# Strided sparse attention with an MLP: loads, scores, half sums and V copies of chunk 1 in another order

## The chip, the core and the metric

The kernel runs on one core of a Trainium2 chip. The metric is the device time of one execution in microseconds. The engines are named as in the profile: PE (matrix multiplies; PEld its weight loads), DVE (vector), ACT (scalar, activations), POOL (GpSimd), SP (it issues DMAs). DMAs issued by POOL go through its software queue, DMAs issued by SP through a hardware queue.

## The reference

Inputs are q, k, v of shape (8, 8, 576, 64) in float32, weights w_in (512 x 2048) and w_out (2048 x 512), and alpha (2048). What matters of the computation:

```python
scores = q @ k.transpose(0, 1, 3, 2) / sqrt(64)
mask_local   = (rel >= 0) & (rel < 32)                      # heads 0 to 3
mask_strided = (rel >= 0) & (pos_k % 32 == pos_q % 32)      # heads 4 to 7
attn = softmax(where(mask, scores, -1e9)) @ v
x = attn.transpose(0, 2, 1, 3).reshape(4608, 512)
h = x @ w_in
out = (maximum(h, 0) + alpha * minimum(h, 0)) @ w_out
```

## The kernel before

The work is one stream on PE with two strands. One strand is the MLP in 9 chunks of 512 tokens (chunk 0 is planned separately). The other is the attention of 32 pairs of heads: pair g belongs to batch g // 4; the first two pairs of a batch are local, the last two strided. The attention of batch n + 1, and the start of the batch after it, runs in between the matmuls of chunk n.

For a pair there are these pieces. T turns q and k of the two local pairs of a batch (PE transposes by identity, copies on ACT). For strided pairs, and from batch 2 on, q and k are loaded in their order by `load_d` (POOL's queue, tiles `qsd` and `ksd`) and turned by `transpose_d` with DMA transposes on SP. S, `score_both`, computes the scores of the pair in two halves: 12 or 16 matmuls into PSUM tiles (`sp`, `sph`), an exp on ACT for each (L400, L406; the exps of the second half are deferred to this and the next attention step), and a multiplication with the mask (L402, L409), on POOL except for pair 11, whose masks run on DVE. P, `pv_piece`, multiplies a group with V (L430), and DVE divides by the row sums (L437, L439) into `x` or `x16s`. P(g, a) is group a of pair g. X, `x_dma` and `x_copy` bring the result into `xT`: by DMA transposes for local pairs and for the first strided pair of a batch (into `xs` first, L469, from which ACT copies, L478), by PE transposes for the second strided pair.

PSUM is tight: the tiles with tag `ps` (T's results, `sph`, `pv`) share three buffers, so a piece may wait until ACT or DVE has read an earlier one.

In chunk n >= 1 the loop at L942 has 30 slots i. Slots 0 to 15 are up-projection blocks, `lin1_piece`: four matmuls of 512 columns into `hps` (L613), ACT's relu into `neg` (L621), DVE's combination into `gT` (L624). Slots 16 to 29 are down-projection blocks, `lin2_fast`: eight matmuls of 256 columns each. They use a fast scheme with seven products instead of eight, which needs sums of halves of `gT` (`g_sum`, L653, tiles `gsum`) and of w_out (`wout_sum`, tiles `wsum`). After each block, `attn_n(cnt, ab)` takes `cnt` attention pieces from the list built at L501 to L575, then the half sums of that slot are issued. For chunk 1 `cnt` and the sums (`early`, L928) are written out by hand, and so are the loads of batch 3 and the copies of its strided V: `load_v(3, False)` fills `vl`, `load_v(3, True)` fills `stv`, `cast_v` copies `stv` to `vs` on POOL, `cast_l` casts q and k on ACT or POOL. `load_d(3)` comes from the list of pieces, behind the last P of group 10.

In chunk 1 the order before is: slot 0 Tq and slot 1 Tk (pairs 8, 9), slot 4 S(8), 6 S(9), 9 P(8,0), 11 P(8,1), 13 P(9,0), 14 S(10), 15 P(9,1), 16 S(11), 17 P(10,0), 18 Tq (pairs 12, 13), 19 P(10,1), 20 Tk, 21 P(10,2), 22 S(12), 23 P(11,0) and so on. P(9,0) stands ahead of S(10) because of L523.

Ahead of chunk 1 stands chunk 0's down-projection, an order written out by hand at L913 to L918: U(kf) multiplies row block kf of w_out into three banks, W(i) does two row blocks for the fourth. U(8) is the first that needs the third quarter of w_out.

Of the kernel before, what the change touches and what calls it, by code (L numbers as in the profile page):

```python
# [32 lines left out]
def kernel(  # L33
# [13 lines left out]
    B, H, S, D = q.shape  # L47
# [36 lines left out]
    DX = 2  # L84
# [404 lines left out]
    def T(u, nm):  # L489
        return lambda: transpose_piece(u, nm)  # L490
# [4 lines left out]
    def Pv(g, i):  # L495
        return lambda: pv_piece(pairs[g], i)

    def X(g, eng=None):
        return lambda: x_piece(pairs[g], eng or ("act" if pairs[g].strided else "dve"))

    for g in range(7, npair + 2):  # L501
        c = g // 4
        a, p, t = g, g - 1, g + 1
        okA = 8 <= a < npair
        okP = 8 <= p < npair
        okT = 8 <= t < npair and t < 4 * NX and (t % 4 == 0 or t < 4 * DX and t % 2 == 0)
        nP = len(pairs[p].pgroups) if okP else 0
        seq = []
        if okA:
            seq.append(("S", lambda a=a: score_both(pairs[a])))  # L510
        if okP:
            seq.append(("P", Pv(p, 0)))
        if okT:
            seq.append(("T", T(t // 2, "q")))
        if 8 <= g - 2 < npair and not pairs[g - 2].xd:
            seq.append(("X", X(g - 2)))
        if okP:
            seq.append(("P", Pv(p, 1)))
        if okT:
            seq.append(("Tk", T(t // 2, "k")))  # L520
        if nP == 3:
            seq.append(("P", Pv(p, 2)))
        if g == 10:  # L523
            seq[0], seq[1] = seq[1], seq[0]
        if not seq:
            seq.append(("N", lambda: None))

        todo = [(c, pr) for pr in range(2)] if g % 4 == 0 and 8 < g < npair else []

        if g % 4 == 1 and 9 <= g and c + 1 < B:  # L530
            todo = [(c + 1, nm) for nm in "qk"]
        lastP = max([i for i, z in enumerate(seq) if z[0] == "P"], default=len(seq) - 1)
        nslots = [i for i, z in enumerate(seq) if z[0][0] != "S"] or list(range(len(seq)))
        for i, (kind, fn) in enumerate(seq):
            extra = []
            if todo and i in nslots:
                left = len([z for z in nslots if z >= i])
                cnt = -(-len(todo) // max(1, left))
                extra = [todo.pop(0) for _ in range(min(cnt, len(todo)))]

            def run(fn=fn, extra=extra, g=g, c=c, kind=kind, lastp=(i == lastP), first=(i == 0),
                    second=(i == min(1, len(seq) - 1))):
                fn()
                for b, pr in extra:
                    if pr in ("q", "k"):
                        if b == 3:
                            continue
                        if b < NX:
                            cast_l(b, pr)
                        if b + 1 < NX:  # L550
                            load_qk(b + 1, pr)
                        continue
                    if b == 3:
                        continue
                    cast_v(b, pr, "pool")
                    if pr == 1 and b + 1 < B:
                        load_v(b + 1, True)
                if first and g % 4 == 2 and NX <= c + 1 < B:
                    turn_rows(c + 1)
                if lastp and g % 4 == 3 and NX <= c + 2 < B:  # L560
                    load_rows(c + 2, "k")
                if lastp:
                    if 4 * DX <= g - 1 < npair and pairs[g - 1].xd:
                        x_dma(pairs[g - 1])
                    if g % 4 == 3 and DX < c + 1 < B:
                        transpose_d()
                    if g % 4 == 2 and DX <= c and c + 1 < B:
                        load_d(c + 1)
                    if g % 4 == 1 and DX < c and c + 1 < B:
                        load_v(c + 1, False)  # L570
                    if g % 4 == 1 and NX <= c + 2 < B:
                        load_rows(c + 2, "q")
                if second and 4 * DX <= g - 3 < npair and pairs[g - 3].xd and pairs[g - 3].strided:
                    after.append(lambda: x_copy(pairs[g - 3]))
            feed(run, g - 2 if kind == "X" else -1)  # L575
# [247 lines left out]
    def ov(b, eng, c0, c1):  # L823
        return lambda: over_v(b, eng, c0, c1)
# [54 lines left out]
    def U(kf):  # L879
        def run():  # L880
            if kf == 0:
                banks.extend(phpool.tile([128, 512], F32, tag="hps", name="ops") for _ in range(3))
            for mt in range(3):
                keep(nc.tensor.matmul(  # L884
                    banks[mt], gTs[0][:, kf, 128 * mt : 128 * mt + 128], wout16[:, kf, :],
                    start=(kf == 0), stop=(kf == 15)))
            if kf == 15:
                for mt in range(3):
                    osb = opool.tile([128, 512], F32, tag="osb", name="osb")
                    cast_copy("dve" if mt == 1 else "act", osb, banks[mt])  # L890
                    keep(nc.sync.dma_start(out[128 * mt : 128 * mt + 128, :], osb))
        return run

    def W(i):
        def run():
            if i == 0:
                ops_cur["t"] = pspool.tile([128, 512], F32, tag="ps", name="ops")
            for kf in (2 * i, 2 * i + 1):
                keep(nc.tensor.matmul(  # L899
                    ops_cur["t"], gTs[0][:, kf, 384:512], wout16[:, kf, :], start=(kf == 0), stop=(kf == 15)))  # L900
            if i == 7:
                osb = opool.tile([128, 512], F32, tag="osb", name="osb")
                keep(nc.scalar.copy(osb, ops_cur["t"]))
                keep(nc.sync.dma_start(out[384:512, :], osb))
        return run

    def ws(z):
        return lambda: wout_sum(z, "dve", 0)

    def sc1(g, eng="dve"):  # L910
        return lambda: score_both(pairs[g], eng)

    for fn in [  # L913
        vs(1, 0, "pool"), sc1(6), U(0), vs(1, 1, "pool"), U(1), sc1(7), U(2), U(3), Cl(1, "q", "act"), Pv(6, 1),
        Cl(1, "k"), Pv(6, 2), Pv(6, 0), U(4), U(5), Pv(7, 0), Pv(7, 1), U(6), loads2, T(2, "q"), U(7), Pv(7, 2), W(0), W(1),
        T(2, "k"), U(8), X(7, "act"), U(9), ws(0), ws(1), ws(2), W(2), sc1(4), W(3), ov(1, "dve", 0, 24), U(10), sc1(5, "pool"), W(4), U(11),
        X(6, "act"), Pv(4, 1), W(5), Cl(2, "q", "act"), Cl(2, "k", "act"), U(12), Pv(4, 0), U(13), Pv(5, 0), U(14), Pv(5, 1),
        U(15), W(6), X(4, "dve"), X(5, "dve"), W(7)]:  # L918
        fn()
    for z in range(3):  # L920
# [5 lines left out]
    load_qk(3, "k")  # L926

    early = {  # L928
        11: [(0, 0, "pool")], 16: [(0, 1, "dve"), (1, 0, "dve")], 18: [(1, 1, "dve"), (2, 0, "dve")],
        20: [(2, 1, "dve"), (3, 0, "dve")], 22: [(3, 1, "dve")]}  # L930
    sums = {
        5: [(2, 0, "pool")], 9: [(0, 0, "pool")], 16: [(0, 1, "dve"), (1, 0, "dve")],
# [5 lines left out]
    for n in range(1, NCH):  # L938
        ab = attn_until(n + 1) if n + 1 < B else len(pieces)
        left = ab - pos["i"]  # L940
        acc = 0.0
        for i in range(30):  # L942
            if i < 16:
                lin1_piece(n, 8 * (i // 8) + 2 * (i % 4) + i % 8 // 4)
            else:
                lin2_fast(n, i - 16)
            if n == 1:
                cnt = int(i > 12 or i in (0, 1, 4, 6, 9, 11))
            else:
                acc += left / (19.5 if n == B - 2 else 21) * (0.5 if i < 16 else 1.0)  # L950
                cnt = int(acc)
                acc -= cnt
            attn_n(cnt, ab)
            for z, h, eng in {1: early, 2: sums2}.get(n, sums).get(i, ()):
                g_sum(n, z, h, eng)
            if n > 1:
                continue
            if i == 7:
                for pr in range(2):
                    cast_v(2, pr, "pool")  # L960
                    load_qk(4, "qk"[pr])
            if i == 15:
                load_v(3, False)
                load_v(3, True)
                cast_l(3, "q", "act")
            if i == 17:
                cast_l(3, "k", "act")
            if i == 28:
                for pr in range(2):
                    cast_v(3, pr, "pool")  # L970
                load_v(4, True)
        while pos["i"] < ab:
            attn_step(ab)
# [30 lines left out]
```

## Time and profile before

| what | value |
| --- | --- |
| runs | 300.34, 298.74, 298.70 us; median 298.74 |
| profiled execution | 298.81 us, its span in the profile 296.9 us |
| granted TensorE clock | 0.999 |
| busy share of the span | PE 98%, PEld 63%, DVE 73%, ACT 61%, POOL 62% |
| DMA | 41.18 MB in 97488 packets, mean 139 GB/s |
| the chain that ended last, by engine | PE 75%, DMA 13%, DVE 5%, ACT 2%, POOL 2% |

A timeline row of the profile reads: start in us, time in us, engine, line, operation, out<-in, shapes, count; in brackets the idle time of that engine just before and what ended it. Times of matmuls overlap, since they are pipelined and their ends are modelled. L numbers are lines of the kernel before.

### The profile page before, as it was taken

What the parts mean: (1) busy time and instruction counts of PE and PEld (TensorE: products, weight loads), DVE (VectorE), ACT (ScalarE), POOL (GpSimd) and SP (SyncE); (2) the same over time, 40 slices, a digit from 0 to 9 for tenths busy, and PEclk for the clock granted to TensorE, in tenths of its full rate; (3) what the DMA queues carried; (4) which work ended last, traced back from release to release, by engine and by line L of the source; (5) the groups of instructions that cost most, each with busy time, mean ns of one, the idle gap of its engine ahead of it and who ended that gap; (6) DMA issues with size and microseconds to landing.
All of it is one profiled execution on the core that took longest, in us unless ns stands there. A gap on an engine that the chain in (4) does not pass through costs nothing.

```text
span 296.9 us, 6949 instructions
## 1 busy us (share of the span) xinstructions
PE 290.0 (98%) x2732; PEld 187.5 (63%) x2732; DVE 217.5 (73%) x412; ACT 182.4 (61%) x337; POOL 183.1 (62%) x167
## 2 busy tenths in 40 slices
PE   8999999999899999999999999999999999999995
PEld 2764554544786478646864687468745964784484
DVE  4687886669976887589848984898489848926852
ACT  1677766797857775776477647764676357416730
POOL 8462536998739999979896987595563305002300
PEclk9999999999999999999999999999999999999999
DMA  7999999999997999999999999997711130022004
GB/s 180 257 193 202 233 202 246 209 169 343 102 141 212 126 127 93 173 184 145 160 192 127 138 133 181 173 113 93 200 21 23 34 132 0 0 73 71 0 2 142
DMA packets 97488, 41.18 MB, mean 139 GB/s; under 512 B 75360, under 2 KB 94256, under 8 KB 97456
## 3 DMA queue, kind: packets, MB, share of 16 engines
q0 software_dynamic: 51008, 17.77, 62.8%
q1 hardware_dynamic: 46096, 22.32, 38.7%
q10 hardware_dynamic: 352, 0.66, 0.9%
q8 instruction: 21, 0.34, 0.5%
q14 instruction: 11, 0.09, 0.1%
HBM read 38.24 MB, written 9.44 MB: 161 GB/s over the span
## 4 chain that ended last, share of the span: by engine, by line
PE 75%; DMA 13%; DVE 5%; ACT 2%; POOL 2%; issue 2%; ACTq 0%; DVEq 0%; POOLq 0%
PE hps L613 34%; PE ops L719 23%; PE ops L709 8%; DMA win<-in_moe_w_in_dram 7%; DMA wout<-in_moe_w_out_dram 6%; PE pv L430 3%; PE sp L377 2%; PE ops L884 2%; DVE gsum L653 2%; DVE gT L624 1%; PE sph L377 1%; PE ops L899 1%; PE xp L455 1%; ACT neg L621 1%; POOL win L754 1%
## 5 line engine op out<-in xcount | busy, mean ns | idle before, releaser
L613 PE MATMUL hps<-xT,win 128*128 128x512 f16 x576 | 132.7, 380 | 0.1
L624 DVE SCALAR_TENSOR_TENSOR gT<-neg,oma,hps 128x512 f16<-128x512 f32 x144 | 105.3, 744 | 35.8 <-ACT neg L621 28.2
L621 ACT ACTIVATE neg<-hps 128x512 f32<-128x512 f32 x144 | 86.1, 600 | 34.7 <-PE hps L613 32.0
L613 PEld LDWEIGHTS <-win 128*128 128x128 f16 x576 | 53.4, 98 | 58.1 <-issue 0.4
L653 POOL TENSOR_TENSOR gsum<-gT 128x1024 f16<-128x1024 f16 x15 | 31.8, 2122 | 41.7 <-DVE gT L624 36.7
L402 POOL TENSOR_TENSOR et<-et,consts 128x576 f16<-128x576 f16 (+1 forms) x23 | 33.0, 1433 | 29.7 <-ACT et L400 29.4
L719 PEld LDWEIGHTS <-gT 128*128 128x128 f16 x384 | 35.7, 97 | 6.0 <-issue 0.3
L439 DVE TENSOR_TENSOR x<-pv,rc 96x384 f16<-96x384 f32 (+2 forms) x62 | 33.0, 532 | 2.1
L719 PE MATMUL ops<-wout,gT 128*128 128x256 f16 x256 | 32.1, 273 | 0.1
L709 PE MATMUL ops<-wsum,gsum 128*128 128x256 f16 x248 | 30.7, 273 | 0.8 <-DVE gsum L653 0.8
L409 POOL TENSOR_TENSOR et<-et,consts 128x576 f16<-128x576 f16 (+1 forms) x23 | 30.1, 1310 | 0.1
L430 PEld LDWEIGHTS <-et 72*128 72x128 f16 (+1 forms) x448 | 23.6, 98 | 9.1 <-DVE x16s L439 0.5
L709 PEld LDWEIGHTS <-gsum 128*128 128x128 f16 x256 | 23.6, 97 | 4.0 <-DVE gsum L653 1.1
L400 ACT ACTIVATE et<-sp 128x576 f16<-128x576 f32 (+1 forms) x24 | 15.5, 647 | 16.5 <-PE sp L377 16.5
L719 PEld LDWEIGHTS <-gsum 128*128 128x128 f16 x256 | 23.7, 98 | 3.0
L664 DVE TENSOR_TENSOR osb<-ops,par 128x512 f32<-128x512 f32 (+1 forms) x16 | 10.8, 675 | 16.9 <-PE ops L719 9.4
L437 DVE RECIPROCAL rc<-pv 72x6 f32<-72x6 f32 (+2 forms) x80 | 14.7, 184 | 9.5 <-PE pv L430 9.2
L662 ACT COPY osb<-ops 128x512 f32<-128x512 f32 x16 | 9.4, 587 | 16.5 <-PE ops L719 16.3
L406 ACT ACTIVATE et<-sph 128x288 f16<-128x288 f32 (+1 forms) x48 | 19.1, 412 | 0.0
L736 ACT COPY par<-ops 128x512 f32<-128x512 f32 x15 | 8.8, 588 | 13.1 <-PE ops L709 12.6
L719 PE MATMUL ops<-wsum,gsum 128*128 128x256 f16 x128 | 16.2, 273 | 0.0
L719 PE MATMUL ops<-wsum,gT 128*128 128x256 f16 x128 | 16.1, 273 | 0.0
(112 smaller groups left out, 356.0 us busy)
## 6 DMA issues: line engine op xcount, KB each, us to landing
out_dram<-osb SPq DMA_DIRECT2D x35, 256.0 KB, 3.1
vl<-in_v_dram POOLq DMA_DIRECT2D x6, 384.0 KB, 10.4
win<-in_moe_w_in_dram POOLq DMA_DIRECT2D x4, 512.0 KB, 17.3
wout<-in_moe_w_out_dram POOLq DMA_DIRECT2D x4, 512.0 KB, 18.5
qsd<-in_q_dram POOLq DMA_DIRECT2D x7, 288.0 KB, 5.9
ksd<-in_k_dram POOLq DMA_DIRECT2D x7, 288.0 KB, 7.4
stv<-in_v_dram POOLq DMA_DIRECT2D x7, 288.0 KB, 7.5
ql<-in_q_dram SPq DMA_DIRECT2D x3, 576.0 KB, 6.5
```

Source lines behind the costliest of these rows:

```text
L400: keep(nc.scalar.activation(ev.rearrange("r (y c) -> r y c", y=2), sp[0:r, :, 0:n], AF.Exp, scale=SCALE))
L402: keep(mul(mv, mv, m, op=ALU.mult))
L406: keep(nc.scalar.activation(ev[:, n * y : n * y + n], sps[y][0:r, 0:n], AF.Exp, scale=SCALE))
L409: keep(mul(mv, mv, m, op=ALU.mult))
L430: keep(nc.tensor.matmul(pv[:, 65 * x : 65 * x + 65], et[0:r, c : c + 128], v16[0:r, 2 * P.pr + hh, t, :] if P.strided else v16[:, 6 * (2 * ...
L439: keep(nc.vector.tensor_tensor(P.x16[0:w, c0 : c0 + 64 * nb].rearrange("r (c e) -> r c e", e=64), pvv[:, :, 0:64], rc[0:w, 0:nb].unsqueeze ...
L613: keep(nc.tensor.matmul(hps, win16[:, kk, 128 * m : 128 * m + 128], xT[:, kk, c0 : c0 + 512], start=(kk == (0 if n else 2)), stop=(kk == ( ...
L621: keep(nc.scalar.activation(neg, hps, AF.Relu, scale=-1.0))
L624: keep(nc.vector.scalar_tensor_tensor(gTs[n][:, m, :], neg, oma[:, m : m + 1], hps, op0=ALU.mult, op1=ALU.add))
L653: keep((nc.vector if eng == "dve" else nc.gpsimd).tensor_tensor(gsum[i][:, hs], a, b, op=op))
L709: keep(nc.tensor.matmul(o, gsum[i][:, y, 128 * z : 128 * z + 128], wsum[i][:, y, :], start=(x == "5" and y == 0 and (z == 0 or alone)), st ...
L719: keep(nc.tensor.matmul(o, lhs(y), rhs(y), start=(first and y == 0), stop=(y == 7), skip_group_check=True))
```

## The change

Six things are placed elsewhere; nothing is added or left out, and each engine has the same number of instructions.

1. In the order of chunk 0's down-projection, W(2) moves from behind the sums of w_out to ahead of U(8).
2. In chunk 1 the second attention piece (Tk of pairs 8, 9) comes in slot 2 instead of slot 1.
3. The exchange at L523 goes: S(10) comes in slot 13 and P(9,0) in slot 14. P(9,1) stays in slot 15.
4. `load_d(3)` no longer comes from the list of pieces, but in slot 15 of chunk 1, and the V loads there change their order. On POOL the order was: mask of S(10), qsd, ksd, second mask of S(10), vl, stv; it becomes: both masks, stv, vl, qsd, ksd.
5. The sums (0, second half) and (1, first half) on DVE move from slot 16 to slot 15, so they stand ahead of pair 11's first mask on DVE instead of behind it.
6. The two copies of the strided V of batch 3 and the load of batch 4's move from slot 28 to slot 24: on POOL they stand ahead of pair 13's masks and of the casts of batch 4's q and k between them, instead of behind.

```diff
-        if g == 10:
-            seq[0], seq[1] = seq[1], seq[0]
...
-                    if g % 4 == 2 and DX <= c and c + 1 < B:
+                    if g % 4 == 2 and DX < c and c + 1 < B:
                         load_d(c + 1)
...
-        T(2, "k"), U(8), X(7, "act"), U(9), ws(0), ws(1), ws(2), W(2), sc1(4), W(3), ...
+        T(2, "k"), W(2), U(8), X(7, "act"), U(9), ws(0), ws(1), ws(2), sc1(4), W(3), ...
...
-        11: [(0, 0, "pool")], 16: [(0, 1, "dve"), (1, 0, "dve")], 18: [(1, 1, "dve"), (2, 0, "dve")],
+        11: [(0, 0, "pool")], 15: [(0, 1, "dve"), (1, 0, "dve")], 18: [(1, 1, "dve"), (2, 0, "dve")],
...
-                cnt = int(i > 12 or i in (0, 1, 4, 6, 9, 11))
+                cnt = int(i > 12 or i in (0, 2, 4, 6, 9, 11))
...
             if i == 15:
+                load_v(3, True)
                 load_v(3, False)
-                load_v(3, True)
+                load_d(3)
                 cast_l(3, "q", "act")
             if i == 17:
                 cast_l(3, "k", "act")
-            if i == 28:
+            if i == 24:
                 for pr in range(2):
                     cast_v(3, pr, "pool")
                 load_v(4, True)
```

More of the change, by code (lines that the diff above doesn't have):

```diff
@@ L915 @@
         Cl(1, "k"), Pv(6, 2), Pv(6, 0), U(4), U(5), Pv(7, 0), Pv(7, 1), U(6), loads2, T(2, "q"), U(7), Pv(7, 2), W(0), W(1),
-        T(2, "k"), U(8), X(7, "act"), U(9), ws(0), ws(1), ws(2), W(2), sc1(4), W(3), ov(1, "dve", 0, 24), U(10), sc1(5, "pool"), W(4), U(11),
+        T(2, "k"), W(2), U(8), X(7, "act"), U(9), ws(0), ws(1), ws(2), sc1(4), W(3), ov(1, "dve", 0, 24), U(10), sc1(5, "pool"), W(4), U(11),
         X(6, "act"), Pv(4, 1), W(5), Cl(2, "q", "act"), Cl(2, "k", "act"), U(12), Pv(4, 0), U(13), Pv(5, 0), U(14), Pv(5, 1),
```

## The prediction

> **What bounds the kernel now.** I read the profile's page first (TensorE is busy nearly all the time), then the busy time by window, with windows cut at the first up-projection matmul of each chunk, then who waited for whom, and last the timeline of each engine. The windows of chunks 1, 2 and 3:
>
> ```profile
> 56.33:91.23 34.90, 33.76 (x364) 22.59 (x363) 26.42 (x50) 27.22 (x52) 27.16 (x20) 1.00 1.40 197
> 91.23:122.58 31.35, 31.10 (x316) 21.07 (x314) 24.36 (x44) 21.55 (x41) 31.28 (x30) 1.00 1.24 135
> 122.58:152.52 29.94, 29.94 (x299) 20.00 (x297) 22.84 (x44) 18.70 (x35) 26.64 (x25) 1.00 1.45 172
> ...
> ```
>
> After the length come the busy times of PE, weight loads, DVE, ACT and POOL, then the granted clock (1.00). PE is the bound: chunk 3 has no idle time at all, chunk 2 has 0.25 us and chunk 1 has 1.14 us. So a change in chunk 1 can give back only what PE waits for there, and it must not make PE wait later. The PE timeline where chunk 1 turns from up- to down-projection:
>
> ```profile
> 71.05 0.35 PE L430 MATMUL pv<-vl,et 128*128 128x65 f16 x6
> ...
> 72.19 0.30 PE L377 MATMUL sp<-qT,kT 64*128 64x72 f16 x8
> ...
> 72.55 1.04 PE L613 MATMUL hps<-xT,win 128*128 128x512 f16 x4
> 73.77 0.34 PE L430 MATMUL pv<-vl,et 128*128 128x65 f16 x6 [0.18 <-ACT et L406]
> ...
> 74.92 0.31 PE L377 MATMUL sp<-qT,kT 64*128 64x72 f16 x8
> ...
> 76.17 0.35 PE L430 MATMUL pv<-vs,et 72*128 72x65 f16 x6
> 76.36 1.04 PE L709 MATMUL ops<-wsum,gsum 128*128 128x256 f16 x8
> 77.23 0.67 PE L292 MATMUL tp<-consts,ql 128*128 128x128 f16 x9
> 78.50 1.05 PE L709 MATMUL ops<-wsum,gsum 128*128 128x256 f16 x8 [0.60 <-DVE gsum L653]
> 79.79 0.36 PE L430 MATMUL pv<-vs,et 72*128 72x65 f16 x6 [0.25 <-DVE x16s L439]
> ```
>
> Ends of matmuls are modelled, so I price by starts. Eight matmuls of 256 columns take 76.36 to 77.23, 0.87 us for 2048 columns; four of 512 take the same, nine transposes of 128 then take 0.49, six pv 0.19, a score block 0.36 (72.19 to 72.55). Hence three stalls: before 73.77 (1.22 - 0.87 = 0.35), before 78.50 (1.27 - 0.49 = 0.78), before 79.79 (1.29 - 0.87 = 0.42): 1.55 us. Their causes on ACT, DVE and POOL:
>
> ```profile
> 73.32 0.40 ACT L406 ACTIVATE et<-sph 72x288 f16<-72x288 f32 x1
> 74.41 1.15 ACT L230 CAST ql<-ql 128x1152 f16<-128x1152 f32 x1
> 75.45 0.65 ACT L400 ACTIVATE et<-sp 72x576 f16<-72x576 f32 x1
> 76.00 0.41 ACT L406 ACTIVATE et<-sph 72x288 f16<-72x288 f32 x1
> ```
> ```profile
> 75.14 0.55 DVE L439 TENSOR_TENSOR x<-pv,rc 96x384 f16<-96x384 f32 x1
> 76.14 1.70 DVE L402 TENSOR_TENSOR et<-et,consts 72x576 f16<-72x576 f16 x1 [0.44 <-ACT et L400]
> 77.76 0.68 DVE L653 TENSOR_TENSOR gsum<-gT 128x1024 f16<-128x1024 f16 x1
> ...
> 79.18 0.55 DVE L439 TENSOR_TENSOR x16s<-pv,rc 72x384 f16<-72x384 f32 x1
> 79.66 0.45 DVE L409 TENSOR_TENSOR et<-et,consts 72x576 f16<-72x576 f16 x1
> ```
> ```profile
> 70.58 2.12 POOL L653 TENSOR_TENSOR gsum<-gT 128x1024 f16<-128x1024 f16 x1
> ...
> 74.72 0.78 POOL L135 DMA_DIRECT2D qsd<-in_q_dram  x1
> ...
> 76.23 1.28 POOL L409 TENSOR_TENSOR et<-et,consts 72x576 f16<-72x576 f16 x1
> ...
> 78.96 0.75 POOL L212 DMA_DIRECT2D stv<-in_v_dram  x1
> 84.47 1.27 POOL L402 TENSOR_TENSOR et<-et,consts 128x576 f16<-128x576 f16 x1 [4.77 <-ACT et L400]
> ```
>
> The pv at 73.77 follows the exp that empties a score bank by 0.05 us (73.32 + 0.40). The second stall is the sum at 77.76, queued on DVE behind pair 11's mask; that mask waited for its exp and then took 1.70 us, where the same shape at 79.66 takes 0.45, because POOL ran pair 10's second mask beside it (76.23 to 77.51). That mask was late because two load issues stood ahead of it. The third stall is DVE again: the bank of P(10,0) is released by x16s at 79.73.
>
> **The change part by part**, on the clock of before. *W(2) ahead of U(8).*
>
> ```profile
> 44.61 0.67 PE L292 MATMUL tp<-consts,kl 128*128 128x128 f16 x9
> 45.83 0.81 PE L884 MATMUL ops<-wout,gT 128*128 128x512 f16 x3 [0.55 <-DMA wout<-in_moe_w_out_dram]
> ```
>
> PE is through with the transposes at 45.10 and U(8) waits for its quarter of the weights until 45.83. W(2) is two matmuls of 512 columns on a quarter that is already in use: 0.44 us, all inside the 0.73 us gap. Gain 0.43; nothing between there and 56.33 is paced by a load that the shift would meet on PE. Without that cover it gives 0.
>
> *The k transposes of pairs 8 and 9 one up-projection block later* (slot 1 to slot 2). No instruction more. ACT drains one more bank first; I take 0.10 gain, between 0 and 0.2: the window has 1.14 us idle, and 1.03 of it stands in the three tags above.
>
> *Pair 10's scores from slot 14 to 13, P(9,0) behind them.* The scores now start at 71.05; behind them come a block, P(9,0), and a block (0.36 + 0.87 + 0.19 + 0.87), so P(9,1) comes at 73.34 with its bank long empty: the 0.35 is gone there. But the order of banks moves the same wait on: P(10,0), for which PE is ready at 73.34 + 0.19 + 0.87 + 0.36 + 0.87 = 75.63, now takes the bank of pair 11's first half. On ACT the q cast stands ahead of pair 11's exps and comes forward by only 0.38 (it follows the neg of the last up-projection block, which ends at about 74.03), so that exp ends at 76.00 + 0.41 - 0.38 = 76.03 and P(10,0) starts at 76.08: 0.09 earlier than before, not 0.54. Queued behind it on PE: everything.
>
> *Loads behind the masks.* POOL is free of its sum at 72.70, so pair 10's masks run 72.70 to 75.25 instead of ending at 77.51. Then stv, vl, qsd, ksd are issued without a mask between them.
>
> *First-half sums ahead of pair 11's mask* (slot 15). On DVE they follow pair 9's last x, which falls to about 76.2 (one more gT stands ahead of it), so two sums of 0.68 end by 77.5. PE wants the first at 76.08 + 0.19 + 0.87 + 0.49 = 77.63: the 0.78 stall is gone. The mask follows at 77.5 with POOL only issuing loads beside it (the sums at 77.76 took 0.68 beside such issues): 0.45. Then rc and x16s to 78.66, so P(10,1) starts at about 78.72, where PE is ready at 78.50. Against 79.79 that is 1.07; I take 1.05. Bounds: 79.97 if the mask takes 1.70 again (loss 0.2), and 78.1 if neither it nor P(10,0) waits (gain 1.7). Who waits for the later mask: only P(11,0), in slot 23.
>
> *V copies of batch 3 from slot 28 to 24* (two copies, one load issue, on POOL). They need stv, issued first now, 9 us ahead of them. POOL was idle 4.77 us before 84.47, so about 2.8 us moved there delays pair 13's masks by little, and these are used in chunk 2 only; POOL's backlog in chunk 2 shrinks by the same. Cost nothing; if stv were late, pair 13's masks would follow it.
>
> *The next deadline: pair 10's output.* It goes by a DMA transpose (xs), two ACT copies, and the first block of chunk 2:
>
> ```profile
> 83.78 1.21 SPq L469 DMA_TRANSPOSE xs<-x16s  x1
> ...
> 87.64 2.60 SPq L176 DMA_TRANSPOSE kT<-ksd  x1
> ```
> ```profile
> DMA to landing us min/median/max: 6.0/6.0/6.0
> ```
> ```profile
> 89.77 1.40 ACT L478 COPY xT<-xs 128x384 f16<-128x384 f16 x2 [0.32 <-DMA xs<-x16s]
> 91.07 0.69 ACT L230 COPY xT<-xp 128x384 f16<-128x384 f16 x2
> ```
> ```profile
> 91.23 2.75 PE L613 MATMUL hps<-xT,win 128*128 128x512 f16 x12
> ```
>
> xs lands 6.0 us after its issue, 89.78, and ACT waits for it. The copies end at 91.76 and PE's fourth matmul wants them at 91.23 + 3 x 0.22 = 91.88: 0.12 us of slack. With PE 1.58 earlier (0.43 + 0.10 + 1.05), xs must land by 88.31. If its 6.0 us stay, it lands at 88.2: no stall. If it lands only once POOL's loads have drained, those start when they did before (75.25 - 0.53 = 74.72) but, with no mask of 1.28 between them, are all issued about 1.2 us sooner, so it lands 1.2 us earlier, 88.6: stall 0.3. If it does not come forward at all: stall 1.4. I take 0.2. The Trainium skill (DMA: Bandwidth & Descriptors, Queues, rings and completion order) says that each DMA engine takes turns between the queues with work, a packet at a time; by that xs keeps its 6.0 us and the sum would be 0.2 lower. No row here shows the turns themselves.
>
> *Chunk 2.*
>
> ```profile
> 112.83 1.05 PE L709 MATMUL ops<-wsum,gsum 128*128 128x256 f16 x8 [0.25 <-DVE gsum L653]
> ```
> ```profile
> 110.08 2.70 DVE L653 TENSOR_TENSOR gsum<-gsum,gT 128x1024 f16<-128x1024 f16 x2
> ```
>
> Two sums took 2.70 instead of 1.36, beside POOL masks. POOL, less behind, runs these masks earlier: gain up to 0.25, or the overlap falls on the sum before, loss up to 0.7 (half of 1.34). I take a gain of 0.1.
>
> **Sum.** The profiled execution took 298.81 us (span 296.9), 0.07 from the median 298.74, so no correction. 298.81 - 0.43 - 0.10 - 1.05 + 0.20 - 0.10 = 297.33: **297.3 us**, -0.5%. In chunk 3 PE is never idle, and the chunks behind it are ordered alike, so I let a shift pass to the end unchanged.
>
> **The rivals.** *A. More comes off* (chance 0.2): P(10,0) does not wait, xs keeps up, chunk 2's stall goes: 0.43 + 0.10 + 1.7 + 0.25 = 2.5, 296.3 us; with the rest of the 0.2 of the k transposes and some of what modelled ends hide, 296.0. For it: the three stalls sum to 1.55 by starts. Against: the bank order, and the cast on ACT.
>
> *B. Given back at chunk 2's start* (0.17): xs lands no earlier than 89.78. PE starts the block's fourth matmul at 91.88 as before: 298.7 us. For it: ACT already waits 0.32 there. Against: its input is ready 1.6 us sooner. If instead the mask on DVE stays at 1.70 the time is about 298.5; I count that here.
>
> *C. Slower: the strided q and k of batch 3 come too late* (0.13). They are now last in POOL's queue and stand behind the V loads, and one more V load is issued ahead of their transposes' end. The flight of the last of the four loads of before (stv, issued at 78.96), and the flight of the k transposes over the run:
>
> ```profile
> DMA to landing us min/median/max: 9.0/9.0/9.0
> ...
> DMA to landing us min/median/max: 3.4/4.6/8.9
> ```
>
> If ksd, now the last, lands where stv did, at 87.9, the k transpose is issued there; at 8.9 it lands at 96.8. Pair 14's scores stand behind five up-projection blocks and a pv of chunk 2, 91.23 + 5 x 0.87 + 0.19 = 95.8, now 94.3. PE stalls 2.5: 299.8 us. It decides from a landing past 94.3. For it: the queue order. Against: at 4.6 it lands at 92.5.
>
> **How the numbers follow.** Forecast 0.5, A 0.2, B 0.17, C 0.13. About 1% (3.0 us) is what a measurement of this kernel can tell from no change. The stalls here hold less than that, so faster by over 1% (below 295.8) needs the far end of A and something unseen: 0.12. Slower by over 1% (above 301.8) needs C with a second late landing: 0.08. Within 1%: 0.80. The range of 296.0 to 299.8 reaches from A to C; the forecast's own is 296.7 to 298.0.
>
> **What would show it.** Right: the wait of PE on gsum in chunk 1 gone, pair 11's first mask on DVE near 0.45 us, pair 10's second mask ending before any load issue, a short wait of P(10,0) on pair 11's exp, chunk 1 about 33.8 us long, W's two matmuls ahead of the weight wait. Wrong: ACT waiting over 1 us for xs, PE waiting for kT from DMA in chunk 2, or any idle PE in chunks 3 to 5.

## The result, and the profile after

The kernel after took 301.37 us (median of 22 runs, 297.75 to 310.04) against 298.27 us (22 runs, 297.6 to 300.34) for the kernel before: ratio 1.0066, 95% interval 1.0043 to 1.0088. It is slower, by 0.7% as the ratio has it and by 1.0% between the medians: a small loss, but the interval keeps clear of 1. The forecast was 297.3 us, and 301.4 lies above the range of 296.0 to 299.8. The ratio leaves out the executions more than 1.5% above the fastest of their kernel, so it is nearer to 1 than the quotient of the medians. The profiled execution took 300.42 us (span 298.6, granted clock 1.0) against 298.81 (span 296.9).

L numbers above 523 are two lower than in the kernel before. The windows of chunks 1, 2 and 3 of the kernel after, cut at the first up-projection matmul of each chunk as before:

```profile
55.35:89.31 33.96, 33.52 (x364) 22.57 (x364) 25.09 (x50) 25.64 (x49) 29.30 (x23) 1.00 1.43 188
89.31:124.23 34.92, 31.25 (x317) 21.03 (x315) 22.98 (x44) 22.88 (x43) 28.11 (x27) 1.00 1.10 151
124.23:154.17 29.94, 29.94 (x299) 20.05 (x297) 22.84 (x44) 18.70 (x35) 26.69 (x25) 1.00 1.34 155
```

Chunk 1 starts 0.98 us earlier (55.35 for 56.33) and is 0.94 shorter (33.96 for 34.90). Chunk 2 is 3.57 longer (34.92 for 31.35), with 3.67 us in which PE is idle. The balance at the start of chunk 3 is +1.65 us, and the two profiled executions differ by 1.61: all of it is here. The PE timeline of chunk 1's middle and of chunk 2's start:

```profile
75.02 0.34 PE L430 MATMUL pv<-vs,et 72*128 72x65 f16 x6 [0.16 <-ACT et L406]
75.20 1.04 PE L707 MATMUL ops<-wsum,gsum 128*128 128x256 f16 x8
76.08 0.67 PE L292 MATMUL tp<-consts,ql 128*128 128x128 f16 x9
76.58 1.04 PE L707 MATMUL ops<-wsum,gsum 128*128 128x256 f16 x8
77.45 0.35 PE L430 MATMUL pv<-vs,et 72*128 72x65 f16 x6
...
89.31 0.59 PE L611 MATMUL hps<-xT,win 128*128 128x512 f16 x2
93.11 0.38 PE L611 MATMUL hps<-xT,win 128*128 128x512 f16 x1 [3.21 <-ACT xT L478]
93.94 2.10 PE L611 MATMUL hps<-xT,win 128*128 128x512 f16 x9 [0.46 <-ACT xT L230]
```

The three stalls of chunk 1 are gone but for 0.16 us (another 0.27 us, at 87.12, is a wait of P(12,0) for vl). In their place stands one of 3.21 + 0.46 us: PE waits for ACT's copies of pair 10's output (L478) and for the copies that ACT does behind them (L230). DVE, POOL, SP and ACT of the kernel after show why:

```profile
74.78 0.68 DVE L651 TENSOR_TENSOR gsum<-gT 128x1024 f16<-128x1024 f16 x1
75.38 0.68 DVE L651 TENSOR_TENSOR gsum<-gsum,gT 128x1024 f16<-128x1024 f16 x1
75.98 0.45 DVE L402 TENSOR_TENSOR et<-et,consts 72x576 f16<-72x576 f16 x1
```
```profile
72.65 1.27 POOL L409 TENSOR_TENSOR et<-et,consts 72x576 f16<-72x576 f16 x1
73.87 0.77 POOL L212 DMA_DIRECT2D stv<-in_v_dram  x1
74.64 1.47 POOL L222 DMA_DIRECT2D vl<-in_v_dram  x1
76.10 0.73 POOL L135 DMA_DIRECT2D qsd<-in_q_dram  x1
76.83 0.71 POOL L135 DMA_DIRECT2D ksd<-in_k_dram  x1
```
```profile
81.16 1.20 SPq L469 DMA_TRANSPOSE xs<-x16s  x1
...
92.12 1.39 ACT L478 COPY xT<-xs 128x384 f16<-128x384 f16 x2 [5.03 <-DMA xs<-x16s]
```

xs is issued at 81.16, 2.6 us earlier than before, and ACT gets it at 92.1, 2.3 us later. The DMA issues of this stretch, with the KB of each and the median time from issue to landing, before and then after (after, the view puts stv together with batch 4's, so its line is left out; this stv lands first, at 79.3):

```profile
vl<-in_v_dram POOLq DMA_DIRECT2D x1, 384.0 KB, 10.2
qsd<-in_q_dram POOLq DMA_DIRECT2D x1, 288.0 KB, 5.8
ksd<-in_k_dram POOLq DMA_DIRECT2D x1, 288.0 KB, 7.4
stv<-in_v_dram POOLq DMA_DIRECT2D x1, 288.0 KB, 9.0
...
xs<-x16s SPq DMA_TRANSPOSE x1, 6.0
```
```profile
vl<-in_v_dram POOLq DMA_DIRECT2D x1, 384.0 KB, 12.3
qsd<-in_q_dram POOLq DMA_DIRECT2D x1, 288.0 KB, 12.3
ksd<-in_k_dram POOLq DMA_DIRECT2D x1, 288.0 KB, 13.4
...
xs<-x16s SPq DMA_TRANSPOSE x1, 10.9
```

The last of the four loads lands at 76.83 + 13.4 = 90.2 (before: stv, 78.96 + 9.0 = 88.0), though the first was issued 0.9 and the last 2.1 us sooner. From the first issue to the last landing the group took 16.3 us instead of 13.2. The engines did what was planned; the DMAs did not follow.

### The profile page after: what moved, and what is told of

It reads as the page before. It is cut to its first block, busy times and chain, and to the rows that moved or that the text cites. A ratio compares the mean times of both kernels' runs of the same rounds, so it can differ in the third digit from the quotient of the medians.

```text
span 298.6 us, 6947 instructions
## 1 busy us (share of the span) xinstructions
PE 289.9 (97%) x2732; PEld 187.8 (63%) x2732; DVE 215.2 (72%) x412; ACT 182.2 (61%) x337; POOL 182.2 (61%) x167
## 4 chain that ended last, share of the span: by engine, by line
PE 84%; DMA 7%; DVE 4%; ACT 1%; issue 1%; POOL 1%; SPq 1%; DVEq 0%; ACTq 0%; POOLq 0%
PE hps L611 40%; PE ops L717 21%; PE ops L707 8%; PE pv L430 4%; DMA xs<-x16s 4%; PE ops L882 4%; DMA ql<-in_q_dram 3%; PE sp L377 2%; PE ops L897 1%; DVE gsum L651 1%; DVE gT L622 1%; PE xp L455 1%; PE sph L377 1%; PE tp L292 1%; DVE x L439 1%
## 5 line engine op out<-in xcount | busy, mean ns | idle before, releaser
L402 POOL TENSOR_TENSOR et<-et,consts 128x576 f16<-128x576 f16 (+1 forms) x23 | 32.5, 1414 | 33.3 <-ACT et L400 33.0
L409 POOL TENSOR_TENSOR et<-et,consts 128x576 f16<-128x576 f16 (+1 forms) x23 | 29.7, 1291 | 0.1
L437 DVE RECIPROCAL rc<-pv 72x6 f32<-72x6 f32 (+2 forms) x80 | 14.7, 184 | 10.3 <-PE pv L430 10.0
L660 ACT COPY osb<-ops 128x512 f32<-128x512 f32 x16 | 9.4, 587 | 16.5 <-PE ops L717 16.3
```

The source lines that it names most:

```text
L402: keep(mul(mv, mv, m, op=ALU.mult))
L409: keep(mul(mv, mv, m, op=ALU.mult))
```

## The experiments

The first theory was that the group of four loads of slot 15 sets when xs lands, and that its new order or batch 4's load (moved to slot 24) made it late. The rivals were that one of the two edits alone does it, that xs is slow by itself, and that the forecast gain on PE isn't there. Each kernel was compared with the kernel before on the same chip; on the four chips used the kernel before had medians of 298.08, 298.09, 298.07 and 298.19 us. Kernels that ran on different chips are compared by these ratios.

**1. Batch 4's load back in slot 28**, the order of slot 15 as after.

```diff
             if i == 24:
                 for pr in range(2):
                     cast_v(3, pr, "pool")
+            if i == 28:
                 load_v(4, True)
```

> The changed kernel with one thing undone: the load of batch 4's strided V goes back from slot 24 to slot 28; the two copies of batch 3's V stay in slot 24. Theory Q (the pair 10 transpose xs lands only when POOL's software queue has drained, and the moved load keeps that queue busy for about 4 us more): xs lands by about 90.2 us, when the last of the four slot 15 loads has landed, instead of 92.1; ACT's wait for it falls from 5.0 to about 3 us, PE's from 3.7 to about 1.8 us, time about 298.5 us. Rival O (the order of the four slot 15 loads alone delays xs): xs still lands near 92, no change, about 300.4 us in a run like the profiled one. Rival P (PE is merely earlier at a fixed date of xs): no change either.

301.69 us, ratio 1.0065 (1.0030 to 1.0099): as slow as the change. xs still lands late (82.85 + 9.1 = 91.95), behind ksd (78.41 + 11.7 = 90.1). That the moved load alone delays xs falls. A second thing stands in this profile, read in the last section. (This execution began chunk 1 at 57.19, 1.8 us later than the kernel after, so its times are not to be set beside that kernel's one by one.)

**2. The order of slot 15 turned to qsd, ksd, stv, vl**, batch 4's load in slot 24.

```diff
             if i == 15:
-                load_v(3, True)
-                load_v(3, False)
                 load_d(3)
+                load_v(3, True)
+                load_v(3, False)
```

> The changed kernel with the loads of slot 15 in the order qsd, ksd, stv, vl (strided q, k first again, still behind both masks of pair 10); the moved load stays in slot 24. Theory Q: the queue holds the same bytes and drains at the same time, xs still lands at about 92 and the time stays at 300 to 301 us. Rival O: qsd and ksd land near 82 us as before, the transposes of batch 3 and xs go early, xs lands near 88, PE's wait falls under 0.5 us, time about 297.2 us.

300.08 us, ratio 1.0006 (0.9970 to 1.0041): no difference from before can be told. Now vl is last and late, and PE waits for it in P(12,0), ahead of chunk 2:

```profile
90.23 0.49 PE L430 MATMUL pv<-vl,et 128*128 128x65 f16 x6 [3.79 <-DMA vl<-in_v_dram]
```

**3. Both: that order, and batch 4's load in slot 28** (the two diffs above together).

> Both together: slot 15 loads in the order qsd, ksd, stv, vl and batch 4's load in slot 28; all else as in the changed kernel (W(2), Tk, pair 10's scores, the sums, the copies in slot 24). Theory Q: as with the load alone put back, about 298.5 us. Rival O: as with the order alone, about 297.2 us. If both count, 297.2 us here and more in each of the other two. Rival P: 300.4 us still.

298.00 us, ratio 1.0025 (0.9990 to 1.0059): the time of before. PE waits 0.9 us for vl and 0.5 for the copies, as the waits of this profile say:

```profile
PE pv L430 <- DMA vl<-in_v_dram: 0.9, 1, 0.9
PE hps L611 <- ACT xT L230: 0.5, 1, 0.5
```

The group ends at 76.00 + 11.6 = 87.6 and xs lands at 81.19 + 8.2 = 89.4, hardly before the 89.8 of before. Even here what PE gains in chunk 1 is given back around chunk 2's start, as the forecast's rival B has it; but the longer of the two waits is for vl, which B did not name.

**4. The kernel before with the two edits of POOL's queue alone** (items 4 and 6 of the change).

```diff
-                    if g % 4 == 2 and DX <= c and c + 1 < B:
+                    if g % 4 == 2 and DX < c and c + 1 < B:
...
             if i == 15:
+                load_v(3, True)
                 load_v(3, False)
-                load_v(3, True)
+                load_d(3)
...
-            if i == 28:
+            if i == 24:
```

> The kernel before with only the load part of the change: strided q, k of batch 3 behind pair 10's masks and behind the V loads, copies of V and batch 4's load in slot 24. PE's own order is untouched, so xs is issued near 83 us as before. Theory Q: xs lands near 92 or later instead of 89.8, PE waits 2 to 3 us at the start of chunk 2, time 300.5 to 301.5 us, and it scatters. Rival P (the shift of PE is what makes xs late): no wait, about 298 us, a little under before since the second mask of pair 10 ends sooner.

300.52 us (4 runs), ratio 1.0104 (1.0062 to 1.0145). The loss comes with the DMA edits alone, and nothing of PE's order is needed for it:

```profile
92.15 0.38 PE L613 MATMUL hps<-xT,win 128*128 128x512 f16 x1 [2.11 <-ACT xT L478]
```

**5. The kernel before with the other four edits alone** (items 1, 2, 3 and 5: all lines of the change's diff that are not in the one above).

> The kernel before with the four edits of PE's and DVE's order alone (W(2), the k transposes, pair 10's scores, the first-half sums); the loads, their order and the V copies as before. Theory 1 (the loads set a floor for xs and vl, and the gain of the edits is given back at chunk 2's start): 297.6 to 298.5 us, with ACT waiting over 1 us for xs. Theory 2 (the gain of 1.6 us passes, only the loads' new order costs): 296.5 to 297.3 us.

299.20 us, ratio 1.0043 (1.0019 to 1.0067): 0.7 us above the range of the first theory, and 1.9 above the second's. ACT waits 3.1 us for xs (81.43 + 9.0 = 90.4), and PE 1.3 us for vl and 0.2 + 0.5 for the copies. The last load, stv, was issued 1.9 us sooner than before (77.05 for 78.96) and landed 0.6 us later (88.6 for 88.0). So the gain on PE does not pass with the loads in their old order either: issued sooner, the group did not end sooner.

**6. The kernel after with pair 10's output turned on PE**, so that no xs exists.

```diff
-        P.xd = P.b >= DX and P.hp < 3
+        P.xd = P.b >= DX and P.hp < 3 and g != 10
```

> The kernel after, with pair 10's output turned by PE transposes (as pair 11's already is) instead of the DMA transpose xs. Theory 1 (the late landing of xs is all that costs): the 3.7 us that PE waits for ACT's copies of xs are gone, about 0.3 us of transposes are added on PE and one more drain each on ACT: about 297.0 us, and no wait of PE over 0.5 us at chunk 2's start. Theory 2 (the whole group of loads is late, xs is only the first to show it): the wait goes over to another transfer of the group, vl for P(12,0) or kT for pair 14's scores, and the time is 298.5 to 300.

297.34 us, ratio 0.9962 (0.9941 to 0.9984): about 1.0% below the change by the ratios, and faster than before. With xs out of the way no other transfer of the group stops PE for more than 0.3 us, and at chunk 2's start PE waits 0.14 us for an ACT copy. (This profile has one wait of 1.1 us, at chunk 1's start, for another ACT copy; that is ahead of all these loads.) The late xs is what costs the change its loss, and the forecast gain in chunk 1 is there.

**7. Both V loads of batch 3 in slot 3**, only q and k in slot 15, batch 4's load in slot 28.

```diff
+            if i == 3:
+                load_v(3, True)
+                load_v(3, False)
...
             if i == 15:
-                load_v(3, True)
-                load_v(3, False)
                 load_d(3)
```

> The kernel after, with batch 3's two V loads issued in slot 3 of chunk 1 instead of slot 15, only the strided q and k left in slot 15, and batch 4's strided V load back in slot 28 (the copies stay in slot 24). Theory 1 (the four loads and the transposes share one drain that ends near 89 us, and xs is behind it): with half of the loads out of that stretch xs lands within about 6 us of its issue, by 87.5, vl is there long before, PE does not wait at chunk 2's start, and the time is 296.0 to 297.0 us. Theory 2 (xs takes 8 to 11 us there whatever stands in POOL's queue, since it shares the transposes' own queue): xs still lands at 89 or later and the time is 298 to 300.

296.65 us (5 runs), ratio 0.9944 (0.9924 to 0.9963). xs lands 4.9 us after its issue, at 87.6, and PE waits for neither xs nor vl. The theory that xs takes 8 to 11 us whatever stands in POOL's queue falls. The early loads have a price of their own: PE now waits 0.36 us for the k transpose of batch 2, ahead of pair 10's scores.

**8. The same with batch 4's load in slot 24** (`load_v(4, True)` stays behind the copies).

> As the kernel after with batch 3's V loads in slot 3, but batch 4's strided V load stays in slot 24. Theory 1 (it is the bytes queued at one time that delay xs): with two of the four loads gone the load of slot 24, issued behind xs, finds little in the queue, and the time equals that of the kernel with it in slot 28, 296.0 to 297.2. Theory 2 (a load issued between xs's issue and its landing delays it by itself): xs lands 1 to 2 us later than in that kernel and the time is 1 us or more above it.

297.18 us, ratio 0.9972 (0.9955 to 0.9988). The intervals touch those of number 7, so a cost of the slot is not shown; if there is one, it is about half a us. The profiled execution was the slowest of the ten (298.65), and not through xs: ahead of pair 10's scores PE waits for the k transpose of batch 2, which is in flight while the two early V loads are and lands at 72.5 instead of 68.2 in the kernel after.

```profile
PE sp L377 <- DMA kT<-ksd: 2.4, 1, 2.4
```

**9. Only vl in slot 3**, and **10. only stv in slot 3**, batch 4's load in slot 24 in both. These were to tell bytes from vl's small packets.

```diff
+            if i == 3:
+                load_v(3, False)   # number 10: load_v(3, True)
...
             if i == 15:
                 load_v(3, True)    # number 10: load_v(3, False)
-                load_v(3, False)
                 load_d(3)
```

> The kernel after with only the local V load (vl, 3072 packets of 128 B, 384 KB) moved to slot 3; stv, qsd and ksd stay in slot 15 and batch 4's load in slot 24. Theory 1a (the drain goes by bytes): 864 KB are left, at the 120 KB per us of the profiles some 7.2 us, so the last of them lands near 83 to 84, xs within 6 us of its issue, and the time is that of both early, 296.7 to 297.5 us. Theory 1b (the drain goes by the small packets of vl): the same result, since these are gone; the two are told apart by the kernel with stv early. Theory 3 (neither matters; ksd standing last in the queue is the trouble): ksd lands at 88 or later, xs behind it, and the time is 299 to 301.

> The kernel after with only the strided V load (stv, 288 packets of 1 KB, 288 KB) moved to slot 3; vl, qsd and ksd stay in slot 15 and batch 4's load in slot 24. Theory 1a (bytes): 960 KB are left, the drain ends about 2.4 us earlier than in the kernel after (87.8 instead of 90.2), xs lands near 89.5, and the time is 298 to 299 us. Theory 1b (vl's small packets): the drain ends as late as in the kernel after, 89 to 90, xs lands at 91 to 92, and the time is 300 to 301.5. Theory 3: as 1b.

297.06 us, ratio 0.9964 (0.9952 to 0.9976), and 297.15 us, ratio 0.9969 (0.9951 to 0.9987). Number 9 took the expected time, though its last load landed at 85.6 and not at 83 to 84. Number 10 came out better than any theory had it: the group ends at 76.74 + 9.0 = 85.7, not 87.8, and xs lands at 85.9. vl's packets were all there, so they are not the trouble as such; nor do 288 KB less explain 4.5 us. What number 10 also did was to put vl first in the group. In its profile PE waits 1.2 us for the k transpose of batch 3 in chunk 2, the wait that the forecast's rival C looked for; in number 9's it does not.

**11. Numbers 7 and 6 together** (both diffs).

> Both V loads early and batch 4's load back in slot 28, and in addition pair 10's output turned by PE transposes instead of xs. Theory 1 (with the loads early xs is no longer in the way): nothing is left to gain from taking xs off, and the transposes cost PE some 0.3 us: 296.7 to 297.1 us, not below the kernel with xs. Theory 2 (xs still costs in the runs that are not profiled): 296.0 to 296.5.

297.88 us, ratio 0.9997 (0.9984 to 1.0011): 1.2 us worse than with xs, not the 0.3 expected. Once the loads are out of the way, turning the output on PE gains nothing. Why it costs 1.2 us is not shown: the only profile is of the slowest execution (303.25; the other nine took 297.55 to 299.37), and what it shows is again the k transpose of batch 2:

```profile
73.55 0.42 PE L377 MATMUL sp<-qT,kT 64*128 64x72 f16 x8 [2.94 <-DMA kT<-ksd]
```

**12. The kernel after once more**, unchanged, for a second profile.

> The kernel after, unchanged, for a second profile of it. Theory 1 (xs cannot land before the group of loads has drained): whatever the time of this execution, xs lands 0.5 to 2.5 us behind the last of the four loads, and PE waits at chunk 2's start by as much as xs lands past 88.3. Theory 2 (xs is slow by itself): xs lands 10 us or more after its issue also where the loads are through earlier.

298.32 us in this execution. xs lands at 81.57 + 8.4 = 90.0, behind ksd at 77.15 + 12.6 = 89.8; PE waits 1.1 + 0.5 us for it. The same program, 2.1 us faster than its first profile, and PE waits 2.1 us less at chunk 2's start (1.55 for 3.67): between these two executions the difference is that of this landing.

**13. and 14. The order of slot 15 alone**, batch 4's load in slot 28 as in number 1: stv, qsd, ksd, vl, and vl, stv, qsd, ksd. Of number 14, against number 1:

```diff
             if i == 15:
-                load_v(3, True)
                 load_v(3, False)
+                load_v(3, True)
                 load_d(3)
```

> The kernel after with the loads of slot 15 in the order stv, qsd, ksd, vl and batch 4's load back in slot 28. Theory Q (q and k must not stand behind vl's 3072 packets): ksd lands by 85, the group ends near 87.6 as in the order qsd, ksd, stv, vl, xs lands near 89.4 and the time is 297.5 to 298.5 us. Theory F (the two loads of V ahead of q and k are the trouble, whichever): stv still first, the group ends at 89 to 90, xs at 91 to 92, and the time is 300 to 302.

> The kernel after with the loads of slot 15 in the order vl, stv, qsd, ksd and batch 4's load back in slot 28. Theory Q (q and k behind vl's packets are late wherever vl stands ahead of them): the group ends at 89 to 90, xs lands at 91 to 92 and the time is 300 to 302 us. Theory S (it is vl standing second that is the trouble, beside pair 9's transposes): the group ends by 88, xs by 89.5, and the time is 297.5 to 298.5.

vl last: 301.43 us, ratio 1.0034 (0.9991 to 1.0076), two executions at 296.7 and 297.3 and eight from 300.4 to 302.7; the ratio settles nothing. In its profile (302.58) vl lands at 91.5 and PE waits 5.0 us for it; xs lands at 91.7. vl first: 297.14 us (7 runs, 296.15 to 298.38), ratio 0.9964 (0.9944 to 0.9984). Number 14 differs from number 1 in nothing but the order of two neighbouring issues, vl ahead of stv instead of behind, and the intervals (0.9944 to 0.9984, and 1.0030 to 1.0099) are far apart: 1.0% between the ratios. The theory that q and k behind vl are late wherever vl stands falls. The issues of the stretch 73 to 91 us in number 1, then in number 14, with the same 4288 packets on POOL's queue (q0: packets, MB, and the time that they took as a share of the stretch of 16 engines):

```profile
q0 software_dynamic: 4288, 1.28, 107.6%
...
vl<-in_v_dram POOLq DMA_DIRECT2D x1, 384.0 KB, 12.1
stv<-in_v_dram POOLq DMA_DIRECT2D x1, 288.0 KB, 5.5
qsd<-in_q_dram POOLq DMA_DIRECT2D x1, 288.0 KB, 11.9
ksd<-in_k_dram POOLq DMA_DIRECT2D x1, 288.0 KB, 11.7
...
xs<-x16s SPq DMA_TRANSPOSE x1, 9.1
```
```profile
q0 software_dynamic: 4288, 1.28, 76.0%
...
vl<-in_v_dram POOLq DMA_DIRECT2D x1, 384.0 KB, 8.7
stv<-in_v_dram POOLq DMA_DIRECT2D x1, 288.0 KB, 9.0
qsd<-in_q_dram POOLq DMA_DIRECT2D x1, 288.0 KB, 10.3
ksd<-in_k_dram POOLq DMA_DIRECT2D x1, 288.0 KB, 10.4
...
xs<-x16s SPq DMA_TRANSPOSE x1, 6.7
```

With vl first the same packets take 76.0% instead of 107.6%, vl itself 8.7 us instead of 12.1, and xs 6.7 instead of 9.1. stv alone lands later (9.0 for 5.5). The kernel before and numbers 2, 3, 5 and 13, which have vl second, third or last, have the same 4288 packets in this stretch at 99.5 to 118.8%, so number 14 stands alone there. The length of the group tells less: from the first issue to the last landing it took 13.4 us in number 14 and 14.7 in number 1 (whose profile is the later one by 1.6 us), 14.2 to 16.3 in the five profiles of the change's order (the kernel after twice and numbers 1, 4 and 6), but 13.2 in the kernel before and 13.8 and 16.6 in numbers 3 and 2, which have one order. One profile does not fix when a group ends.

**15. Only vl in slot 3, and batch 4's load in slot 28** (the diffs of numbers 9 and 1).

> Only the local V load in slot 3 and batch 4's load back in slot 28. With the group 864 KB long xs is through before slot 24, so the place of batch 4's load should not matter: 296.5 to 297.3 us, the same as with it in slot 24 (297.06 us). If the load of slot 24 still costs in the runs that are not profiled, it is 0.5 us or more below that.

296.39 us (8 runs, 295.98 to 297.76), ratio 0.9945 (0.9930 to 0.9961): the lowest median, 0.5% faster than the kernel before and 1.2% below the change by the ratios. Number 7 has the same ratio within the intervals. It is 0.7 us below number 9, but their intervals overlap, so here too a cost of slot 24 is not shown. Its windows of chunks 1 and 2 have 0.25 us and nothing of idle PE:

```profile
55.48:89.26 33.78, 33.53 (x363) 22.54 (x363) 25.58 (x50) 27.56 (x54) 28.89 (x22) 1.00 1.21 200
89.26:120.64 31.38, 31.38 (x318) 21.14 (x316) 23.57 (x44) 21.42 (x41) 28.92 (x29) 1.00 1.28 141
```

Together: when the last load of slot 15 lands and when xs lands (issue plus flight, to 0.1 us, in the one execution that was profiled), and the median time of all executions.

| kernel | last load | xs | median us |
| --- | --- | --- | --- |
| before | stv 88.0 | 89.8 | 298.27 |
| after | ksd 90.2 | 92.1 | 301.37 |
| after, second profile | ksd 89.8 | 90.0 | |
| 1: load 4 in slot 28 | ksd 90.1 | 92.0 | 301.69 |
| 2: order qsd, ksd, stv, vl | vl 90.1 | 89.8 | 300.08 |
| 3: both | vl 87.6 | 89.4 | 298.00 |
| 4: DMA edits alone | ksd 90.5 | 91.1 | 300.52 |
| 5: other edits alone | stv 88.6 | 90.4 | 299.20 |
| 7: both V loads early | ksd 85.0 | 87.6 | 296.65 |
| 8: the same, load 4 in slot 24 | ksd 87.1 | 88.8 | 297.18 |
| 9: vl early | ksd 85.6 | 86.0 | 297.06 |
| 10: stv early | ksd 85.7 | 85.9 | 297.15 |
| 13: vl last | vl 91.5 | 91.7 | 301.43 |
| 14: vl first | ksd 87.2 | 87.8 | 297.14 |
| 15: vl early, load in slot 28 | ksd 85.4 | 85.9 | 296.39 |

xs lands from 0.3 us ahead of the last load to 2.6 us behind it in all 15 profiles that have an xs, whether its flight is 4.1 or 10.9 us. A rival is that xs waits in SP's own queue for pair 9's two transposes, issued ahead of it. These landed from 0.5 to 6.2 us ahead of xs, so they tell its landing less well; that they share in it is not ruled out. Wherever the last load is through by 87.3, the median is 297.2 us or less; wherever it lands later, 298 or more.

## Why the prediction was wrong

**What held.** Chunk 1's steps came as forecast. Pair 10's masks end on POOL before any load issue, the two sums stand ahead of pair 11's mask, and that mask takes 0.45 us instead of 1.70 with POOL only issuing loads beside it. P(10,0) waits shortly for pair 11's exp (0.16). PE no longer waits for the sums, and P(10,1) starts 77.45 - 55.35 = 22.10 us into the chunk where it started at 79.79 - 56.33 = 23.46. The forecast length of chunk 1 was 33.75 us (34.90 less 0.10 and 1.05); it is 33.96 in the kernel after, 0.27 of it the wait for vl, and 33.78 in number 15.

**W(2)**: right in sign, its size not shown. PE no longer waits for the weights:

```profile
44.34 0.67 PE L292 MATMUL tp<-consts,kl 128*128 128x128 f16 x9
44.85 0.59 PE L897 MATMUL ops<-wout,gT 128*128 128x512 f16 x2
45.28 0.81 PE L882 MATMUL ops<-wout,gT 128*128 128x512 f16 x3
```

Of the 0.98 us by which chunk 1 starts earlier, 0.27 were there before this place (44.34 for 44.61). But in number 4, which has W(2) in its old place, chunk 1 started at 55.74 and no wait for the weights is in the trace: the arrival of the weights varies from execution to execution, and so does what the edit is worth. That chunk 1 starts earlier by more than the forecast 0.43 us is in part luck.

**Chunk 2's term** of 0.10 did not come: 31.38 in number 15 against 31.35. The second sum no longer took double (the sums of chunk 2 lie between 0.68 and 0.69 us in the kernel after), but this was worth nothing in length.

**The step that failed** is the term for xs. I took 0.2 us with an upper bound of 1.4; PE waited 3.67. xs was issued even sooner than I forecast (81.16, for 83.78 - 1.58 = 82.20); its flight was wrong, 10.9 us for 6.0. That xs lands about when POOL's loads have drained was one of the two ways weighed, and it fits all the profiles. But I let the drain come forward with the issues ("all issued about 1.2 us sooner, so it lands 1.2 us earlier"), as if the time of the drain depended on its start alone. With the change the four loads were issued 0.9 to 2.1 us sooner and the last landed 2.2 us later. It is not the new order alone: number 5 has the old order, the last load issued 1.9 us sooner and landing 0.6 later. The order adds to it, as numbers 1 and 14 show. And the bound assumed that at worst xs would land where it had landed before. A warning was in the profile of before: the k transposes spread from 3.4 to 8.9 us, so a transfer's flight was not a constant of its size.

The rule cited with this term, that each DMA engine takes turns between its queues (the Trainium skill, DMA: Bandwidth & Descriptors, Queues, rings and completion order), was taken to mean that xs keeps its 6.0 us. The traces do not bear out that conclusion: xs took 10.9 us beside four loads in flight and 4.1 in numbers 9 and 15, so the time of one transfer hung on what lay in the other queue. The turns themselves no run shows.

**A cost that the sum had no term for** is the granted clock. In 12 of the 22 executions of the kernel after the mean clock was 0.994 or less, and these took 299.9 to 310.04 us (median 302.7); the other ten had 0.998 or more and took 297.75 to 301.63 (median 300.5). So with a full clock the late xs leaves the kernel about 2.2 us above the 298.27 of before, and the rest of the 3.1 us between the medians comes with the clock, which the last section reads.

**The rivals.** B, the gain given back at chunk 2's start, was right as a mechanism and too mild: xs landed not as late as before but 2.3 us later. Numbers 3 (298.0) and 5 (299.2) lie on either side of B's own price of 298.7. C named the order of the loads and a ksd landing at 87.9; it landed at 90.2. But its price was looked for in the wrong place: PE was already held by xs, and pair 14's scores did not wait for kT in the kernel after (they did in number 10).

Open is why the same packets take longer when vl is issued behind another load. The small packets alone do not (number 10), nor do the bytes (number 14 has them all). Whether it is where vl's packets meet pair 9's two DMA transposes, which are issued at the same time, or DVE's sums, which run from 74.78 to 76.06 beside vl's issue, wasn't tried.

## What to carry to other kernels

A transfer that becomes ready earlier need not land earlier: take its landing from the end of the group of loads that it runs beside, and give that group's end a range of its own (here 14.2 to 16.3 us for one order). An edit that reorders loads is not free because the same bytes are issued sooner: here two neighbouring issues exchanged are worth 1.0% by the ratios (1.0065 and 0.9964), twice the 0.5% that was forecast for all the edits together. Moving the one load with the most packets to an earlier place was enough here. Look also at what runs in the earlier place: with both V loads there, PE waited 0.4 to 2.9 us for another transpose in all three profiles.

## What the runs showed of the hardware

A stall of PE can cost more than its length, because the granted clock falls behind it. In number 1 PE was idle for 1.74 and 0.46 us, and then the clock was 0.50 for about 3.4 us (0.14 + 3 + 0.26 by the windows from 93 on). Windows (length, busy PE, weight loads, DVE, ACT and POOL, then the clock) and the PE timeline of that kernel:

```profile
91.00:93.00 2.00, 0.27 (x3) 0.01 (x1) 0.00 (x0) 0.99 (x2) 2.00 (x3) 1.00 1.03 149
93.00:94.00 1.00, 0.54 (x2) 0.19 (x2) 0.00 (x0) 1.00 (x4) 1.00 (x3) 0.93 0.85 155
94.00:97.00 3.00, 3.00 (x8) 1.03 (x7) 0.96 (x2) 1.64 (x3) 3.00 (x4) 0.50 0.86 112
97.00:98.00 1.00, 1.00 (x10) 0.52 (x9) 0.53 (x1) 0.35 (x1) 1.00 (x2) 0.87 1.00 116
```
```profile
93.83 3.79 PE L611 MATMUL hps<-xT,win 128*128 128x512 f16 x9 [0.46 <-ACT xT L230]
```

The same nine matmuls took 2.10 us in the kernel after, which had waited longer (3.21 us) and kept its clock at 1.00. Number 2 shows the fall too, from the end of its stall of 3.79 us on:

```profile
90.00:93.00 3.00, 2.77 (x24) 2.24 (x25) 0.75 (x2) 1.26 (x3) 3.00 (x4) 0.50 1.25 265
```

So a like stall costs about 1.7 us more (3.79 for 2.10) in some executions than in others. 3.4 us at half the clock lower the mean of a 300 us execution by 0.006, which is about the 0.993 and 0.994 of eight executions of the kernel after; the 0.982 to 0.989 of four others would be two or three such falls. In number 11's profile the clock was 0.50 for 6.8 us, beginning 2.1 us into PE's idle time ahead of the row of 2.94 us above. In the seven kernels whose medians lie under 297.4 us (numbers 6 to 10, 14 and 15) no execution of the 60 had a mean clock under 0.998, so the falls go with the late landings. They explain a part of the scatter of the kernel after (297.75 to 310.04) beside number 15 (295.98 to 297.76), not all: its ten executions without a fall still spread over 3.9 us, and 310.04 is more than two falls add. The Trainium skill (TensorE: Matmul & The Clock Gate, What's actually happening) tells of half the clock after an idle window of about 3.4 us that runs freely, so that the same kernel may meet it or not. The chance agrees with these runs, and so do the 3.4 us of the fall in number 1; the idle time does not quite, since 2.2 us of it within 2.6 were enough there.
